# Weight gradient stage: x rows first in tiles, twenty full tiles, score gradients turned by the crossbar

## The chip, the cores and the metric

One core of one Trainium2 chip. The metric is device time in microseconds (us) of the whole kernel, median of several executions. All runs below were in the fast state, and every output was correct.

## The reference, cut to what matters

A recurrent attention block (A) gated by a SwiGLU block (B), forward and backward: the kernel returns the output and the gradients of x and of eight weights. Each of 64 segments attends over 8 memory rows and its own 32 rows of x, and its memory is the output of the segment before.

```python
# B=1, S=2048, Dm=640, H=32 heads of 128, M=8 memory rows, seg=32
for s in range(n_seg):
    h = jnp.concatenate([mem, xs], axis=1)          # 40 rows
    q, k, v = [jnp.einsum('btd,dhe->bhte', h, W) for W in (Wq, Wk, Wv)]
    scores = jnp.where(mask, jnp.einsum('bhqe,bhke->bhqk', q, k) * scale, -1e9)
    o = jnp.einsum('bhqk,bhke->bhqe', softmax(scores), v)
    o = jnp.einsum('bhte,hed->btd', o, Wo)
    mem = o[:, :M, :]
...
_out, _vjp = jax.vjp(_f, A_x, A_mem0, A_Wq, A_Wk, A_Wv, A_Wo, B_w1, B_w3, B_w2)
```

The stage of interest comes after the backward recurrence, when P (the probabilities) and dS (the score gradients) of every tile lie in DRAM. It needs the gradients of the v, k and q rows, with them the gradients of Wv, Wk and Wq, and the gradient of the rows of x. The gradient of the memory rows was already needed inside the recurrence, so computing it here again is waste.

## The kernel before

The stage goes over eight groups of four heads (called "quarters" here and in the recorded texts, though there are eight), each with 22 tiles (three segments, 24 memory rows and then 96 rows of x; the last tile has one segment). A pair of quarter and tile is a unit. To turn is to transpose. Per unit: s1 turns dS on TensorE; s2(i) makes the gradient rows r6p of v, k and q (i = 0, 1, 2) in two rotating banks of PSUM (the memory that TensorE writes; a bank is free again when ScalarE or VectorE has emptied it, below an eviction), and the third needs the turned dS (dST); s3 turns these rows (t6g) into a ring; s4 multiplies each full window of 128 rows by the weights (g). After the 22 units, wg makes the three weight gradients from all tiles and from hr, the rows that the heads were computed from.

```python
def s1(u):
    for j in range(4):
        nc.tensor.transpose(pt[:, j, :], dS[0:n, j, :], k.ident[0:n, 0:n])
    nc.vector.tensor_copy(dST[0:n, :, 0:n], pt[0:n])
def s2(u, i):
    pr = pa.tile([P, 512], F32, name="r6p", tag=bank("s", 3, 2))      # banks 3 and 4
    ...                                                               # four products
    # emptied by ScalarE (i = 0, 2) or VectorE (i = 1) into gr
...
for tl in range(NTL):
    u = u0 + tl
    if tl + 4 < NTL: ld(u + 4)
    if tl + 2 < NTL: s2(u + 2, 0); s2(u + 2, 1)
    if tl + 3 < NTL: s1(u + 3)
    if tl + 1 < NTL: s3(u + 1, 0, 2)
    if tl + 2 < NTL: s2(u + 2, 2)
    if tl + 1 < NTL: s3(u + 1, 2, 3)
    s4(u)
...
```

In the timelines of this case each engine's instructions stand in the written order. The queues differ in what issues them: SP issues most loads and all wg stores, ScalarE the g rows' loads (one a unit, between its evictions), GpSimd the memory rows' loads.

Of the kernel before, what the change touches and what calls it, by code (L numbers as in the profile page):

```python
# [16 lines left out]
P = 128  # L17
# [23 lines left out]
class K:  # L41
# [76 lines left out]
    def build_masks(self, pool, scr):  # L118
        nc = self.nc
        GE = ALU.is_ge  # L120
        n, nm = 120, 24
# [7 lines left out]
        for (c0, w) in ((0, 8), (nm, 32)):  # L129
            v1 = a1[:, c0:c0 + 3 * w].rearrange("p (s c) -> p s c", c=w)  # L130
            v2 = a2[:, c0:c0 + 3 * w].rearrange("p (s c) -> p s c", c=w)
            sel(v1, 1, 0, [[-8, 3], [0, w]])
            sel(v1, -1, 7, [[8, 3], [0, w]])
            sel(v2, 1, -nm, [[-32, 3], [0 if w == 8 else -1, w]])
            sel(v2, -1, nm + 31, [[32, 3], [0, w]])
# [8 lines left out]
        sel(b1[:], -1, 7, [[0, 40]])  # L144
        sel(b2[:], 1, 0, [[-1, 40]])
# [6 lines left out]
    def setup_dram(self):  # L152
# [17 lines left out]
        self.GXA = mk("GXA", (self.NR, D))  # L170
# [23 lines left out]
        for tl in range(self.NTL):  # L194
            n = self.geo(tl)[3]
            self.PR.append(mk(f"PR{tl}", (n, H, n)))
            self.DSR.append(mk(f"DSR{tl}", (n, H, n)))
            ns, nm = self.geo(tl)[0:2]
            self.VTD.append(mk(f"VTD{tl}", (P, ns, H, 40)))
        self.PM = mk("PM", (T, P, 80))  # L200

# [25 lines left out]
    def m_src(self, tl, w, c0, c1):  # L227
        g = c0 // 1024
        out, t = [], 3 * tl
        end = t + self.geo(tl)[0]  # L230
        while t < end:
            e = min(end, t - t % 4 + 4)
            XS = self.store(w)[t // 4, g, 0:8, t % 4:t % 4 + e - t]
            for i in range(2 if w == "qv" else 1):
                X = XS[:, :, i] if w == "qv" else XS
                out.append((8 * (t - 3 * tl), 8 * (e - 3 * tl), X[:, :, c0 - 1024 * g:c1 - 1024 * g].rearrange("r t c -> t r c"), i))
            t = e
        return out
# [6 lines left out]
    def m_rows(self, A, t):  # L245
        r = 120 * (t // 3) + 8 * (t % 3)
        return A[r:r + 8, :]

    def x_rows(self, A, X, eng):
        n = self.NTL - 1  # L250
        eng.dma_start(A[0:120 * n, :].rearrange("(t r) d -> t r d", r=120)[:, 24:120],
                      X[0:96 * n, :].rearrange("(t r) d -> t r d", r=96))
        eng.dma_start(A[120 * n + 8:self.NR, :], X[96 * n:self.S, :])


    def x_pieces(self, A, x0, x1):
        out, a = [], x0
        while a < x1:
            tl = a // 96
            b = min(x1, 96 * tl + 96)  # L260
            r = 120 * tl + self.geo(tl)[1] + a - 96 * tl
            out.append((a - x0, b - x0, A[r:r + b - a, :]))
            a = b
        return out
# [103 lines left out]
def phase3_Afwd(k, W4, Wv, Wk_):  # L368
# [30 lines left out]
    with tc.tile_pool(name="ast", bufs=1) as st, tc.tile_pool(name="achain", bufs=1) as ch, \  # L399
# [174 lines left out]
        def ld(w, tl, qd, eng=nc.sync):  # L574
# [4 lines left out]
            k.load_x(r, nm, k.x_src(tl, w, c0, c0 + 512), eng)  # L579
# [11 lines left out]
        def scores(tl, qd):  # L591
# [8 lines left out]
            for j in range(4):  # L600
                kv = kT[:, h0 + j, 0:n].rearrange("p (s c) -> p s c", c=40)
                nc.tensor.matmul(sp[:, j, 0:nm], qT[:, j, :], kv[:, :, 0:8], start=False, stop=True,
                                 skip_group_check=True)
                nc.tensor.matmul(sp[:, j, nm:n], qT[:, j, :], kv[:, :, 8:40], start=False, stop=True,
# [19 lines left out]
        def norm(tl, qd, eng=nc.gpsimd, q=nc.gpsimd):  # L624
# [6 lines left out]
            q.dma_start(k.PR[tl][:, h0:h0 + 4, :], Pb[0:n, :, 0:n])  # L631
# [19 lines left out]
        def pv(tl, qd, q=nc.gpsimd):  # L651
# [3 lines left out]
            if 4 * tl < k.NO:  # L655
                pt = ps.tile([P, 4, 96], F32, name="xot", tag="x", bufs=5)
                for j in range(4):
                    nc.tensor.matmul(pt[:, j, :], v[0:n, j * P:(j + 1) * P], PTs[qd % 2][0:n, j, 24:120], start=True, stop=True)
# [126 lines left out]
def phase3b_out(k, Wo, W0, W4):  # L785
# [12 lines left out]
    with tc.tile_pool(name="oio", bufs=1) as io, tc.tile_pool(name="oac", bufs=1, space=bass.MemoryType.PSUM) as pa, \  # L798
# [6 lines left out]
        def ld(b, qd):  # L805
# [3 lines left out]
            if nt == 3:  # L809
                src = k.OR[120 * tl:120 * tl + 360, c0:c0 + 512].rearrange("(t r) c -> r t c", r=120)[24:120]  # L810
            else:
                nm, n = k.geo(tl)[1], k.geo(tl)[3]
                src = k.OR[120 * tl + nm:120 * tl + n, c0:c0 + 512].rearrange("(t r) c -> r t c", t=1)
# [82 lines left out]
        while g0:  # L896
# [6 lines left out]
    later = [(k.GWO[0:120 * n, :].rearrange("(t r) d -> t r d", r=120)[:, 24:120], k.GS[0:96 * n, :].rearrange("(t r) d -> t r d", r=96)),  # L903
             (k.GWO[120 * n + 8:k.NR, :], k.GS[96 * n:k.S, :])]

    for s in range(3):
# [3 lines left out]
        for b in range(2):  # L910
            r0 = 120 * tl0 + 8 * s
            dst = k.HRO[120 * tl0:120 * tl0 + 120 * (n - 1), :].rearrange("(t r) d -> t r d", r=120)[:, 8 * s:8 * s + 8]
            r1 = 120 * (tl0 + n - 1) + 8 * s
# [3 lines left out]
            later.append((k.HRO[r1:r1 + 8, cols], k.FS[t1, 32 * b:32 * b + 8, :]))  # L917
# [6 lines left out]
def phase4_Abwd(k, out2, WoT, WvT, WkT, WqT, later):  # L924
# [3 lines left out]
    with tc.tile_pool(name="gst", bufs=1) as st, tc.tile_pool(name="gchain", bufs=1) as ch, \  # L928
# [6 lines left out]
        bdf = st.tile([P, 16, 8], BF16, name="bdf")  # L935
        b16 = st.tile([P, 16], F32, name="b16")
        nc.gpsimd.memset(bdf[:], 0.0)
        nc.gpsimd.affine_select(out=bdf[:], in_=bdf[:], compare_op=ALU.not_equal, fill=1.0, base=0,
                                pattern=[[-1, 16], [-16, 8]], channel_multiplier=1)
        nc.vector.tensor_reduce(b16[:], bdf[:], axis=AX.X, op=ALU.add)  # L940
        nc.vector.tensor_copy(bdm[:], bc_last(b16[:], 8))
        goxs = [st.tile([P, DC, 32], BF16, name=f"gox{i}") for i in range(2)]
        gOTs = [st.tile([P, 4, P], BF16, name=f"gOT{i}") for i in range(2)]
        gors = [st.tile([120, 512], BF16, name=f"gor{i}") for i in range(NG)]
        for tt in goxs + gOTs + gors:
# [53 lines left out]
        def chain(t, gap):  # L999
# [76 lines left out]
            with nc.allow_non_contiguous_dma(reason="mem rows of dS"):  # L1076
                for a in range(2):
                    for (c0, c1, d0) in ((0, 8, 8 * s), (8, 40, nm + 32 * s)):
                        (nc.sync, nc.gpsimd)[a].dma_start(k.DSR[tl][8 * s:8 * s + 8, 16 * a:16 * a + 16, d0:d0 + c1 - c0],
# [16 lines left out]
        def ld(tl, qd, eng=None):  # L1096
# [7 lines left out]
            if g < NG:  # L1104
                gor = gors[g][:]
                qv = fl.tile([120, 2, 512], BF16, name="gqv", tag="gqv", bufs=4)[:]
                Pr = fl.tile([120, 4, n], BF16, name="gPr", tag="gPr", bufs=4)[:]
            else:
# [3 lines left out]
                Pr = x[:, 1536:1536 + 4 * n].rearrange("p (h c) -> p h c", h=4)  # L1112
            if gnm.get(g, 0 if g < NG else 1) != 0 and (g >= NG or gnm[g] < nm):
                nc.vector.memset(gor[0:24, :], 0.0)
# [3 lines left out]
            k.load_x(qv, nm, k.x_src(tl, "qv", c0, c0 + 512), nc.sync)  # L1118
            k.load_x(gor, nm, k.g_src(tl, c0, c0 + 512), nc.scalar if early and i > 3 else nc.sync)
# [3 lines left out]
        def turn(tl, qd):  # L1123
# [7 lines left out]
            nc.scalar.copy(vTq[:, :, :, 0:8].rearrange("p s h c -> p h s c"), pt[:, :, 0:nm].rearrange("p h (s c) -> p h s c", c=8))  # L1131
            nc.scalar.copy(vTq[:, :, :, 8:40].rearrange("p s h c -> p h s c"), pt[:, :, nm:n].rearrange("p h (s c) -> p h s c", c=32))
# [8 lines left out]
        def dprob(tl, qd):  # L1141
# [3 lines left out]
            for j in range(4):  # L1145
                nc.tensor.matmul(dp[:, j, 0:nm], gOT[:, j, :], vTq[:, :, j, 0:8], start=True, stop=True)
                nc.tensor.matmul(dp[:, j, nm:n], gOT[:, j, :], vTq[:, :, j, 8:40], start=True, stop=True)
            uu["d", tl, qd] = dp

        def dsoft(tl, qd):  # L1150
# [5 lines left out]
            dS = fl.tile([120, 4, n], BF16, name="gdS", tag="gdS", bufs=2)  # L1156
            for j in range(4):
                nc.vector.tensor_tensor_reduce(dS[0:n, j, :], dp[0:n, j, :], Pr[0:n, j, :], 1.0, 0.0, ALU.mult, ALU.add,
                                               Dx[0:n, j:j + 1])
            for j in range(4):  # L1160
                nc.vector.scalar_tensor_tensor(dS[0:n, j, :], dp[0:n, j, :], Dx[0:n, j:j + 1], Pr[0:n, j, :],  # L1161
# [4 lines left out]
        def gmem(tl, qd):  # L1166
# [5 lines left out]
            for j in range(4):  # L1172
                nc.tensor.matmul(pk[:, 0, j, :], qv[0:n, 0, j * P:(j + 1) * P], dS[0:n, j, 0:nm], start=True, stop=True)
                nc.tensor.matmul(pk[:, 1, j, :], gor[0:n, j * P:(j + 1) * P], Pr[0:n, j, 0:nm], start=True, stop=True)
# [15 lines left out]
        cnt = dict(l=0)  # L1190
# [83 lines left out]
def phase6_Awgrads(k, X, out0, out3, out4, out5):  # L1274

    nc, tc = k.nc, k.tc
    D, DC, S, H, HD, T, NTL = k.D, k.DC, k.S, k.H, k.HD, k.T, k.NTL
    outf = [o.rearrange("d h e -> d (h e)") for o in (out3, out4, out5)]
    out0f = out0.flatten_outer_dims()
    NW = k.NR // P  # L1280
    R = 384
    with tc.tile_pool(name="h6i", bufs=3) as io, tc.tile_pool(name="h6", bufs=1) as hp, \
            tc.tile_pool(name="h6g", bufs=1) as gp, tc.tile_pool(name="h6a", bufs=1, space=bass.MemoryType.PSUM) as pa:
        start = len(nc.cur_bb.bb.instructions)
        hr = hp.tile([120, NTL, D], BF16, name="hr")
        acc = X.tile([P, NW, D], F32, name="ghacc", tag="x")
        NB = 3
        dSs = [hp.tile([120, 4, P], BF16, name=f"dS6{i}") for i in range(NB)]
        Prs = [hp.tile([120, 4, P], BF16, name=f"P6{i}") for i in range(NB)]
        dSTs = [hp.tile([120, 4, P], BF16, name=f"dST6{i}") for i in range(2)]  # L1290
        ring = hp.tile([P, 3, 4, R], BF16, name="gT6")
        for i, tt in enumerate(dSs + Prs + dSTs):
            (nc.gpsimd, nc.vector)[i % 2].memset(tt[:], 0.0)
        units = [(qd, tl) for qd in range(8) for tl in range(NTL)]
        st, Ws, cnt = {}, {}, dict(w=0, s=0, x=0, g=0)
# [15 lines left out]
        def ld(u):  # L1311
# [4 lines left out]
            nc.sync.dma_start(dS[0:n, :, 0:n], k.DSR[tl][:, h0:h0 + 4, :])  # L1316
            nc.sync.dma_start(Pr[0:n, :, 0:n], k.PR[tl][:, h0:h0 + 4, :])
            rw = []
            for nm_ in ("g", "q", "k"):
                r = io.tile([120, 512], BF16, name="r6", tag=f"r6{nm_}")  # L1320
                src = k.g_src(tl, c0, c0 + 512) if nm_ == "g" else k.x_src(tl, nm_, c0, c0 + 512)
                k.load_x(r, nm, src, nc.scalar if nm_ == "g" else nc.sync)
# [4 lines left out]
        def s1(u):  # L1327
            qd, tl = units[u]
            n = k.geo(tl)[3]
            dS = st["l", u][0]  # L1330
            pt = pa.tile([P, 4, n], BF16, name="t6", tag=bank("x", 5, 3))
            for j in range(4):
                nc.tensor.transpose(pt[:, j, :], dS[0:n, j, :], k.ident[0:n, 0:n])  # L1333
            dST = dSTs[u % 2]
            nc.vector.tensor_copy(dST[0:n, :, 0:n], pt[0:n])  # L1335

        def s2(u, i):
            qd, tl = units[u]
            n = k.geo(tl)[3]
            dS, Pr, rw = st["l", u]  # L1340
            lh = (Pr, dS, dSTs[u % 2])[i]
            rh = rw[i]
            pr = pa.tile([P, 512], F32, name="r6p", tag=bank("s", 3, 2))
            for j in range(4):
                nc.tensor.matmul(pr[:, j * P:(j + 1) * P], lh[0:n, j, :], rh[0:n, j * P:(j + 1) * P], start=True, stop=True)  # L1345
# [563 lines left out]
```

## Time and profile before

| | before |
|---|---|
| median (range), us | 5568.7 (5560.69 to 5575.1) |
| span of the profiled run, granted clock | 5562.0, 0.952 |
| end of the last sum before the stage | 3380.3 |
| from there to the first wg product | 153.7 |
| seven quarters, first wg to first wg | 1306.6 (mean 186.7) |
| last wg groups | 71.6 |
| rest of the kernel | 649.7 |

The rows below the span add up to it within 0.1 us; they are times of instructions in the trace (the first is the end of the last product on the summed fsum, the others are starts of wg products), and the same five are compared for the other kernels. Beyond what the prediction shows, two lines of the transfers view of one quarter (3720.7 to 3905.6 us, from the second start of wg to the third) will be needed. The first counts packets; the second gives a load of 160 KB into 128 partitions (eo_s, rows for the output) and its median time from issue to landing in us.

```profile
DMA packets 42747, 18.25 MB, mean 99 GB/s; under 512 B 33828, under 2 KB 42156, under 8 KB 42730
...
eo_s<-SR POOLq DMA_DIRECT2D x2, 160.0 KB, 2.9
```

Most packets are small: 960 pieces of 240 B for each unit's dS and P.

### The profile page before, as it was taken

To read this page: it belongs to the slowest core of one execution; us is meant where nothing else is said; L and a number is where in the kernel's file an instruction comes from. 1 tells how busy PE (TensorE), PEld (TensorE's weight loads), DVE (VectorE), ACT (ScalarE), POOL (GpSimd) and SP (SyncE) were. 2 spreads that over 40 slices of the span, in tenths; PEclk is the share of its full clock that TensorE was granted. 3 is DMA by queue.
4 is the path that set the end of the run, shared out by engine and by line. 5 is a ranking of instruction groups with operands and counts; after the bars stand their busy time and mean duration, and the time that the engine had idled before them with its cause. 6 is when DMAs were issued, how large, how long until landed. Compare 5 with 4: busy or idle time off the path is not lost. (4 is left out here: it accounts for less than half of the span.)

```text
span 5562.0 us, 164947 instructions
## 1 busy us (share of the span) xinstructions
PE 4935.7 (89%) x66673; PEld 3152.5 (57%) x67020; DVE 2343.2 (42%) x7398; ACT 1783.4 (32%) x4953; POOL 1570.4 (28%) x2604
## 2 busy tenths in 40 slices
PE   4987888888888677989999997999999999998999
PEld 2554555555555444656666665566556655666665
DVE  5833555555555323444444542233223322311451
ACT  2422555555555322323333332233113312300111
POOL 0000344444444212333333333243224322310000
PEclk9998999999999778999999998999999999999999
DMA  7553455555555686666666666354335433657332
GB/s 252 171 185 90 137 152 153 158 156 162 153 151 143 152 171 155 176 186 184 186 184 178 185 169 130 76 124 99 94 74 126 98 87 83 162 166 188 106 117 92
DMA packets 1126617, 808.27 MB, mean 145 GB/s; under 512 B 672971, under 2 KB 1016679, under 8 KB 1123179
## 3 DMA queue, kind: packets, MB, share of 16 engines
q1 hardware_dynamic: 884995, 555.06, 37.3%
q0 software_dynamic: 91472, 144.46, 9.3%
q10 hardware_dynamic: 149388, 98.17, 6.3%
q8 instruction: 529, 8.67, 0.7%
q14 instruction: 233, 1.91, 0.1%
HBM read 468.47 MB, written 296.78 MB: 138 GB/s over the span
## 5 line engine op out<-in xcount | busy, mean ns | idle before, releaser
L1403 PE MATMUL wg<-gr,hr 120*128 120x512 bf16 (+1 forms) x2640 | 592.9, 386 | 17.3 <-DVE dST L1335 13.1
L1381 PE MATMUL g<-w,gT 128*128 128x320 bf16 x3840 | 548.4, 299 | 0.0
L1403 PEld LDWEIGHTS <-hr 120*128 120x128 bf16 (+1 forms) x2640 | 258.9, 99 | 343.1 <-issue 52.1
L1381 PEld LDWEIGHTS <-gT 128*128 128x128 bf16 x3840 | 368.8, 98 | 136.3
L243 POOL DMA_DIRECT2D r<-GOS x256 | 143.4, 564 | 795.8 <-PE r6p L1345 704.8
L90 DVE CAST wgo<-wg 128x512 bf16<-128x512 f32 x72 | 47.5, 688 | 589.2 <-issue 281.8
L316 PEld LDWEIGHTS <-hx 128*32 128x32 bf16 x7680 | 179.7, 97 | 169.4 <-issue 12.4
L90 DVE CAST stg<-bank 128x512 bf16<-128x512 f32 x256 | 177.0, 692 | 208.4 <-PE bank L316 199.4
L335 PEld LDWEIGHTS <-gkv 128*8 128x8 bf16 x8192 | 189.7, 87 | 107.4 <-DVE gkv L1012 23.8
L619 ACT ACTIVATE xP<-xsp,xnm 120x120 bf16<-120x120 f32 (+1 forms) x704 | 240.5, 376 | 8.5 <-DVE xnm L615 4.5
L1390 DVE TENSOR_TENSOR ghacc<-ghacc,g 128x320 f32<-128x320 f32 x240 | 117.0, 487 | 277.7 <-PE g L1381 277.7
L92 ACT CAST wgo<-wg 128x512 bf16<-128x512 f32 x48 | 25.8, 589 | 640.3 <-PE wg L1403 640.3
L1163 POOL DMA_DIRECT2D DSR<-gdS x176 | 101.6, 577 | 426.5 <-DVE gdS L1161 383.3
L1348 ACT CAST gr<-r6p 120x512 bf16<-120x512 f32 (+1 forms) x176 | 103.3, 587 | 361.7 <-PE r6p L1345 340.8
L668 POOL DMA_DIRECT2D OR<-xv x163 | 94.6, 580 | 418.9 <-ACT xv L667 287.0
L92 ACT COPY gT<-t6g 128x960 bf16<-128x960 bf16 (+5 forms) x216 | 167.0, 792 | 119.9 <-PE t6g L1364 117.0
L630 POOL TENSOR_TENSOR xP<-xP,xrz 120x480 bf16<-120x480 bf16 x163 | 161.8, 992 | 141.0 <-ACT xP L619 96.5
L1161 DVE SCALAR_TENSOR_TENSOR gdS<-gdp,Dx,gPr 120x120 bf16<-120x120 f32 (+1 forms) x680 | 182.7, 330 | 0.0
L1232 PE MATMUL gbank<-WqT,ident 128*128 128x512 bf16 x453 | 159.5, 402 | 20.1 <-issue 12.2
L335 PE MATMUL bank<-Wo,oTm 128*32 128x320 bf16 x4032 | 177.0, 329 | 0.1
L316 PE MATMUL gbank<-WoT,gox 128*32 128x512 bf16 x2560 | 153.6, 387 | 24.6 <-POOL gox L967 21.2
L1364 PE MATMUL t6g<-ident,gr 120*128 120x120 bf16 (+1 forms) x2112 | 172.0, 221 | 3.3 <-DVE wgo L90 2.7
(339 smaller groups left out, 10991.0 us busy)
## 6 DMA issues: line engine op xcount, KB each, us to landing
QVS<-stg SPq DMA_DIRECT2D x128, 256.0 KB
gqv<-QVS SPq DMA_DIRECT2D x108, 192.0 KB
vTt<-VTD SPq DMA_DIRECT2D x64, 320.0 KB
VTD<-gvT POOLq DMA_DIRECT2D x168, 120.0 KB, 3.6
OR<-xv POOLq DMA_DIRECT2D x163, 120.0 KB, 2.5
DSR<-gdS POOLq DMA_DIRECT2D x168, 112.5 KB, 3.4
dS<-DSR SPq DMA_DIRECT2D x168, 112.5 KB
P<-PR SPq DMA_DIRECT2D x168, 112.5 KB
```

Of the source, the lines that this page charges most:

```text
L90: return nc.vector.tensor_copy(out, in_)
L92: return nc.scalar.copy(out, in_)
L243: eng.dma_start(d, src if src.shape[0] > 1 else src[0])
L316: k.nc.tensor.matmul(bank[32 * g:32 * g + 32, :], x[:, dc, :], W[:, dc, c0:c0 + 512], start=(dc == 0), stop=(dc == k.DC - 1), tile_positio ...
L335: k.nc.tensor.matmul(pm[p0:p0 + nq, 0:320], x[:, h, :], W[:, h, 320 * b:320 * b + 320], start=(first and i == 0), stop=(last and i == 15), ...
L619: nc.scalar.activation(Pb[0:n, j, 0:n], sp[0:n, j, :], ACT.Exp, bias=nmx[0:n, j:j + 1], scale=k.scale, accum_out=Z[0:n, j:j + 1])
L630: eng.tensor_tensor(Pb[0:n, :, 0:n], Pb[0:n, :, 0:n], bc_last(rz[0:n], n), ALU.mult)
L1161: nc.vector.scalar_tensor_tensor(dS[0:n, j, :], dp[0:n, j, :], Dx[0:n, j:j + 1], Pr[0:n, j, :], op0=ALU.subtract, op1=ALU.mult)
L1232: nc.tensor.matmul((bA if g in ("W1", "G1", "G2") else bB)[:], k.ident[:], WqT[:, 0, 0:512], start=True, stop=True)
L1364: nc.tensor.transpose(pt[:, i - i0, j, :], st["g", u, i][0:n, j * P:(j + 1) * P], k.ident[0:n, 0:n])
L1381: nc.tensor.matmul(pg[:], ring[:, i, j, r0:r0 + P], Ws[qd][i][:, j, 320 * h:320 * h + 320], start=(i == 0 and j == 0), stop=(i == 2 and j ...
L1403: nc.tensor.matmul(accs[dc][:], hr[0:n, tl, dc * P:(dc + 1) * P], st["g", NTL * qd + tl, i][0:n, :], start=(tl == 0), stop=(tl == NTL - 1))
```

## The change

The intent: compute the rows' gradient for the 2048 rows of x only (16 windows instead of 20), feed wg with 20 tiles of 128 rows instead of 22 of 120, and take the turns of dS from TensorE: a transposing transfer of the DMA engines, from SBUF to SBUF, makes them (the crossbar turn). For this, x rows come first in each tile; dS and P are stored padded to 128 columns (one piece of 1024 B a row instead of four of 240); tiles 20 and 21 go first and their 160 rows are stored to DRAM (GSP) and loaded back as rows 120 to 127 of the twenty others, in the fifth unit of a quarter (`p == 4`). The new layouts reach into earlier stages, with the same order of work on TensorE there. The core, with cuts marked:

```diff
+        def dturn(u):
+            dST = io.tile([P, 4, P], BF16, name="dST6", tag="dST6", bufs=4)
+            turned_load(k, dST[:], st["l", u][0][:].rearrange("p j c -> p (j c)"))   # crossbar, SP queue
-        def s1(u): ...        # turn by TensorE
-        def s2(u, i): ...
+        def s2(u):            # the three groups in a row
+            for i in range(3): ...
+                if tl >= NF:
+                    nc.gpsimd.dma_start(k.GSP[qd, i, r0:r0 + n, :], gr[0:n])
+        def spill(qd):
+            for i in range(3):
+                nc.gpsimd.dma_start(grs[i][120:P, :, :], k.GSP[qd, i].rearrange("(t r) c -> r t c", r=8))
...
-            for tl in range(NTL):
-                n = k.geo(tl)[3]
+            for tl in range(NF):                                    # wg: 20 tiles of 128 rows
...
+        ld_to(4); dturn(1)
+        nc.scalar.dma_start(hr[0:120], ...)                         # 3 MB; before: after the loads of unit 2
+        nc.scalar.dma_start(hr[120:P], ...)
...
+                if p + 3 < NTL:
+                    s2(u + 3)
+                    ld_to(u + 3 + NB)                               # loads five units ahead, was two
+                dturn(u + 4)
+                if p + 2 < NTL:
+                    s3(u + 2)
+                s4(u)
+                if p == 4:
+                    spill(qd)
```

## The prediction

> **What bounds the kernel now.** I read the page first for the engine that is busy, then split the span by stages, then cut the weight gradient stage (3398 to 4912 us, 1514 us, the only stage whose TensorE program the change alters) into its eight equal quarters, one for each group of four heads, then read one unit of work in the timeline, and last the waits. From the page:
>
> ```profile
> PE 4935.7 (89%) x66673; PEld 3152.5 (57%) x67020; DVE 2343.2 (42%) x7398; ACT 1783.4 (32%) x4953; POOL 1570.4 (28%) x2604
> ...
> L1403 PE MATMUL wg<-gr,hr 120*128 120x512 bf16 (+1 forms) x2640 | 592.9, 386 | 17.3 <-DVE dST L1335 13.1
> L1381 PE MATMUL g<-w,gT 128*128 128x320 bf16 x3840 | 548.4, 299 | 0.0
> ...
> L1364 PE MATMUL t6g<-ident,gr 120*128 120x120 bf16 (+1 forms) x2112 | 172.0, 221 | 3.3 <-DVE wgo L90 2.7
> ```
>
> TensorE is the busy engine, and the two costliest groups of the whole kernel, the weight gradient product (wg) and the rows' gradient (g), are both in this stage; neither waits much. The windows view of one quarter, from the first wg product to that of the next quarter:
>
> ```profile
> 3905.61:4090.45 184.84, 176.10 (x1428) 114.27 (x1426) 57.27 (x124) 47.87 (x77) 57.54 (x104) 0.97 0.42 99
> ```
>
> Columns: window, length, busy us (instructions, in merged rows) of PE, PEld, DVE, ACT, POOL, clock, DMA share, GB/s. PE is busy 95% of a quarter, every other engine under 35%, DMA 42%. Seven such quarters last 184.6 to 189.4 us, mean 186.7 (4840.73 - 3534.07 over 7). So TensorE's order of work sets the time. One unit (a tile of three segments, four heads) in the timeline of TensorE:
>
> ```profile
> 4003.86 0.39 PE L1345 MATMUL r6p<-r,P 120*128 120x128 bf16 x4
> 4004.08 0.39 PE L1345 MATMUL r6p<-r,dS 120*128 120x128 bf16 x4
> 4004.31 0.37 PE L1333 MATMUL t<-ident,dS 120*128 120x120 bf16 x4
> 4004.52 0.58 PE L1364 MATMUL t6g<-ident,gr 120*128 120x120 bf16 x8
> 4004.94 0.39 PE L1345 MATMUL r6p<-r,dST 120*128 120x128 bf16 x4
> 4005.16 0.37 PE L1364 MATMUL t6g<-ident,gr 120*128 120x120 bf16 x4
> 4005.37 3.42 PE L1381 MATMUL g<-w,gT 128*128 128x320 bf16 x24
> 4008.63 0.39 PE L1345 MATMUL r6p<-r,P 120*128 120x128 bf16 x4
> ```
>
> Start to start: 0.22 us for four products of 128 columns, 0.21 for four turns of dS (t), 0.63 for twelve turns of the gradient rows (t6g), 3.26 for the 24 products of one g window; 4.77 in all, without a gap. Note that turns and t6g stand between the second r6p group and the third. The r6p results rotate through two PSUM banks, so the third needs the bank of the first, after ScalarE has emptied it. The same three groups without anything between them occur between the wg groups:
>
> ```profile
> 3957.92 0.38 PE L1345 MATMUL r6p<-r,P 120*128 120x128 bf16 x4
> 3958.14 0.39 PE L1345 MATMUL r6p<-r,dS 120*128 120x128 bf16 x4
> 3958.34 0.59 ACT L1348 CAST gr<-r6p 120x512 bf16<-120x512 f32 x1
> 3958.98 0.38 PE L1345 MATMUL r6p<-r,dST 120*128 120x128 bf16 x4 [0.45 <-ACT gr L1348]
> ```
>
> There the third starts 1.06 us after the first instead of 0.45: 0.61 us lost (the bracket says 0.45, because a group's modelled end is later than its last issue).
>
> **What the Trainium skill says.** "TensorE: Matmul & The Clock Gate", section "Wait — 56ns, not 53.3ns?", gives N / 2.4 GHz + about 2.5 ns per warm matmul. The trace agrees: 3.26 us / 24 = 136 ns at 320 columns, 0.63 / 12 = 52.5 ns at 120. So the turns pay for their columns, not for their weights, and 96 columns should take about 42.5 ns (estimate). "Perfetto Trace Analysis", section "Matmuls", says that independent groups should rotate through banks so that the emptying of one overlaps the next; the 1.06 us above shows what two banks for three groups cost. "DMA: Bandwidth & Descriptors", section "Specifications", asks for at least 512 B a transfer: the dS and P loads here land as four 240 B pieces a row and become one of 1024 B. Its section "Latency and other measured facts" gives 261 GB/s for a DMA transpose; 128 KB would be 0.5 us of the queues (estimate from that page; no run here has a turn from SBUF).
>
> **The change part by part.** All per quarter, from the durations above; the order of TensorE's program before this stage is unchanged, row by row.
> - Rows' gradient for x rows only: 2048 rows are 16 windows of 128 instead of 20. 4 x 3.26 = -13.0.
> - Weight gradients over 20 full tiles instead of 22 of 120 (one short): 30 products fewer of 512 columns at 24.0 / 110 = 0.218: -6.5.
> - Turns of dS go to the crossbar: 22 x 0.21 = -4.6, and 0.4 us of VectorE each, which was hidden.
> - t6g with 96 columns: 12 x 10 ns x 22 = -2.6 (estimate from the rate).
> - Waits of the turns for dS loads: from 3604 to 4830 us TensorE waited 15.3 us for dS<-DSR, 6.6 quarters, so 2.3 each. Loads now run five units ahead over the quarter's edge: -2.3.
>
> That is -29.0. What is added on the same path:
> - The new order has all three r6p groups in a row (the compiled order of the changed kernel shows it: third group waits for ScalarE), still with two banks. 17 units of the steady loop, 0.61 each: +10.4. It does not hide: TensorE is in order, and what follows waits behind it.
> - 16 windows over 22 units leave every fourth unit without g products. There ScalarE has two casts (0.59, 0.60) and a copy of 768 columns (about 0.8, from 0.96 at 960) against 1.8 us of TensorE, so the next unit's first cast starts late. Worked through by hand, the third group then starts 1.55 after the first, 0.49 more than 1.06; four such units: +2.0.
> - Between the wg groups one r6p group more queues behind the wgo casts: +2.0 (judged from 2 to 2.7 us waits there now).
>
> Net -29.0 + 14.4 = -14.6 a quarter, x 8 = -117. The spill of the last two tiles (six small stores, three loads of 8 rows) has some 80 us before wg reads it: hidden. The start of the stage (41 us until the first g product, DMA at 0.9 to 1.15) has the same bytes to load: 0. The other stages keep their order; whole-row stores of P, and one load instead of two or three in the last stage, are worth a few us at most. I give back 10 us for the new queue (below): 5564 - 107 = 5457.
>
> **Rivals.** (1) The saving shows in full: the stall is hidden by TensorE's queue. Then -29 x 8 = -232, about 5330. Against it is the measured 1.06 us with ScalarE idle before. (2) The crossbar turn comes late. It is issued when the unit two before has left TensorE, and after four loads of about 0.4 us on the same queue; its result is needed about 9.8 us later, 6.5 where a unit without a window lies between. Loads take some 3 to 4 us here, so there is room, but at the quarter's edges (DMA 0.96 to 1.05 while the w turns run) it may fail. One us in every unit would be 176 us and leave the kernel slower than before; I think a few waits at the edges more likely, and that is the 10 us. (3) DMA becomes the bound: 42% now, fewer pieces for dS and P, one crossbar transfer more; the share should stay under 55%. (4) ScalarE's backlog spreads: its work is 48 us of 185, so it recovers in each window; against.
>
> **Range and chances.** The terms removed are sure to some 15 us; the stall count is sure, its size 0.5 to 0.7 (plus or minus 20 us); the edges plus or minus 30. Range 5410 to 5505. The 2% line is 5453, a few us under my number, so it is near even: faster 0.46, same 0.53, slower 0.01.
>
> **What would show it.** A steady unit with a window should take 5.05 us instead of 4.77 (longer, though it does less), with r6p<-dST waiting about 0.45 for ACT on line of the cast; units without a window near 1.8; g 3072 products, wg 2400, no t group; wg 64.7 a quarter; quarters near 172. In the waits, DMA dS<-DSR gone as TensorE's releaser, ACT the largest one, some 80 us in the idle column over the stage. I am wrong if r6p<-dST waits for a DMA of dST in the steady loop, if t6g still takes 0.63, if the third group starts under 0.7 us after the first, or if a stage before 3398 moves by over 15 us.

## The result, and the profile after

5610.23 us median (5604.01 to 5615.36), against 5568.7 before: ratio 1.0075 (0.0019 either way at 95%), where 5457 was predicted. All ratios here are the mean time of one kernel's fast runs over that of the other's of the same rounds, so not quite the ratio of the medians. The page of the profiled run, its busy times and its costliest groups of the stage:

```profile
PE 4787.0 (85%) x64913; PEld 3029.7 (54%) x65308; DVE 2245.6 (40%) x7110; ACT 1758.4 (31%) x4913; POOL 1562.8 (28%) x2675
...
L1344 PE MATMUL r6p<-r,dST 120*128 120x128 bf16 (+1 forms) x704 | 74.7, 234 | 224.6 <-DMA dST<-dS 121.3
```

TensorE does 149 us less and the kernel is 47 us longer: the third r6p group has 225 us of idle time before it. The parts of the span, against before: the first part +15.3 (3395.6), from there to the first wg +21.8 (175.5), seven quarters +15.4 (1322.0, where 102 less were predicted), last wg groups -7.1, rest +1.4. The seven quarters are six of 182.7 to 187.0 and a last of 209.1. Who held TensorE from 3398 to 5000 us (total us, times, longest), from the waits view:

```profile
PE r6p L1344 <- DMA dST<-dS: 121.3, 30, 7.9
PE r6p L1344 <- ACT gr L1351: 69.0, 128, 2.8
PE r6p L1344 <- ACT grs L1351: 34.1, 12, 28.8
PE r6p L1344 <- DMA r<-KS: 16.3, 1, 16.3
```

The second line is the stall that was predicted (16 a quarter). The first is the late crossbar turn, which was given 10 us. The last two are, but for 5 us, single long waits at the start of the stage. One such turn in the timeline of the sixth quarter:

```profile
4413.35 0.39 PE L1344 MATMUL r6p<-r,P 120*128 120x128 bf16 x4
4413.58 0.39 PE L1344 MATMUL r6p<-r,dS 120*128 120x128 bf16 x4
4414.41 0.38 PE L1344 MATMUL r6p<-r,dST 120*128 120x128 bf16 x4 [0.45 <-ACT gr L1351]
4414.64 0.68 PE L1374 MATMUL t6g<-ident,gr 96*128 96x96 bf16 x12
4415.15 3.42 PE L1389 MATMUL g<-w,ghacc 128*128 128x320 bf16 x24
...
4426.53 0.61 PE L1344 MATMUL r6p<-r,dST 120*128 120x128 bf16 x4 [7.51 <-DMA dST<-dS]
4426.94 1.17 PE L1374 MATMUL t6g<-ident,gr 96*128 96x96 bf16 x12
4427.90 5.48 PE L1389 MATMUL g<-w,ghacc 128*128 128x320 bf16 x24
```

The first five lines are a steady unit exactly as foretold: 5.06 us from start to start, 0.45 of waiting in it. The unit after it waits 7.51 us for its turn, and then everything runs at a lower rate: twelve t6g turns 1.17 instead of 0.68, a g window 5.48 instead of 3.42. That is what the Trainium skill, "TensorE: Matmul & The Clock Gate", section "What's actually happening", calls the cold state, half clock after an idle window of about 3.4 us; this trace agrees: all 16 of the 30 waits that were 3.9 us or longer are followed by slow products. This wait cost 2.7 us more than its own length (the unit took 14.82 us, 9.76 over a steady one, where the wait of 0.45 became one of 7.51). The windows view from the second start of wg to the third shows that the DMA engines do more than the prediction's 55%:

```profile
3756.80:3941.80 185.00, 154.74 (x1208) 97.69 (x1212) 45.21 (x89) 44.66 (x72) 62.72 (x113) 0.94 0.62 121
```

(last three columns: clock, DMA share, GB/s; before 0.97, 0.42, 99). And the transfers view of the same stretch:

```profile
DMA packets 39881, 22.47 MB, mean 121 GB/s; under 512 B 25592, under 2 KB 39043, under 8 KB 39866
...
gr<-GSP POOLq DMA_DIRECT2D x3, 160.0 KB, 11.6
...
eo_s<-SR POOLq DMA_DIRECT2D x2, 160.0 KB, 4.9
```

The three spill loads into eight partitions take 11.6 us each where 160 KB into 128 partitions took 2.9 before, and now takes 4.9. Fewer packets are small (25592 against 33828), since dS and P come in whole rows; without the turns it would be 13624, as the first experiment shows.

### The profile page after: what moved, and what is told of

The parts are those of the page before. It is cut to its first block, busy times and chain, and to the rows that moved or that the text cites. A ratio compares the mean times of both kernels' runs of the same rounds, so it can differ in the third digit from the quotient of the medians.

```text
span 5608.7 us, 161247 instructions
## 1 busy us (share of the span) xinstructions
PE 4787.0 (85%) x64913; PEld 3029.7 (54%) x65308; DVE 2245.6 (40%) x7110; ACT 1758.4 (31%) x4913; POOL 1562.8 (28%) x2675
## 5 line engine op out<-in xcount | busy, mean ns | idle before, releaser
L1410 PE MATMUL wg<-gr,hr 128*128 128x512 bf16 x2352 | 532.6, 386 | 16.5 <-DVE grs L1353 7.6
L1389 PE MATMUL g<-w,ghacc 128*128 128x320 bf16 x3072 | 471.8, 314 | 0.0
L1410 PEld LDWEIGHTS <-hr 128*128 128x128 bf16 x2400 | 237.9, 99 | 305.0 <-issue 35.8
L1389 PEld LDWEIGHTS <-ghacc 128*128 128x128 bf16 x3072 | 309.8, 103 | 129.9
L1344 PE MATMUL r6p<-r,dST 120*128 120x128 bf16 (+1 forms) x704 | 74.7, 234 | 224.6 <-DMA dST<-dS 121.3
L1398 DVE TENSOR_TENSOR ghacc<-ghacc,g 128x320 f32<-128x320 f32 x192 | 93.7, 488 | 251.0 <-PE g L1389 251.0
L1344 PEld LDWEIGHTS <-dST 120*128 120x128 bf16 (+1 forms) x704 | 55.0, 103 | 247.4 <-DMA dST<-dS 151.1
L1351 ACT CAST gr<-r6p 120x512 bf16<-120x512 f32 x160 | 94.0, 588 | 295.1 <-PE r6p L1344 294.9
```

The costliest lines, as they stand in the source:

```text
L1344: nc.tensor.matmul(pr[:, j * P:(j + 1) * P], lhs[i][0:n, j, :], rw[i][0:n, j * P:(j + 1) * P], start=True, stop=True)
L1389: nc.tensor.matmul(pg[:], ring[:, i, j, r0:r0 + P], Ws[qd][i][:, j, 320 * h:320 * h + 320], start=(i == 0 and j == 0), stop=(i == 2 and j ...
L1410: nc.tensor.matmul(accs[dc][:], hr[:, tl, dc * P:(dc + 1) * P], grs[i][:, tl, :], start=(tl == 0), stop=(tl == NF - 1))
```

## The experiments

Each edit is against the changed kernel. The table lists the result of each as a ratio to the kernel before, and in per cent of it what that is against the changed kernel (1.0075). 0.1% is 5.6 us. The four calls shared their runs of before, whose medians were 5568.0, 5580.3, 5573.1 and 5570.0. The 95% intervals of these ratios reach 0.0017 to 0.0038 either way, so differences under some 0.4% between two rows of the table are not sure.

| run | edit to the changed kernel | median, us | ratio to before | against changed |
|---|---|---|---|---|
| e_peturn | dS turned by TensorE | 5511.88 | 0.9909 | -1.7 |
| e_early | crossbar turn issued 2 units earlier | 5604.33 | 1.0080 | 0.0 |
| e_order | third r6p group after 8 turns | 5574.37 | 1.0018 | -0.6 |
| e_gxa | last-quarter stores off SP | 5577.7 | 1.0025 | -0.5 |
| e_hr | hr later, GpSimd | 5607.05 | 1.0049 | -0.3 |
| e_spill | spill loads spread | 5590.2 | 1.0023 | -0.5 |
| e_x_all | crossbar + all five mends above | 5578.33 | 0.9995 | -0.8 |
| e_x_sp | e_x_all + g rows on SP | 5494.64 | 0.9870 | -2.0 |
| e_pe_order | TensorE turn + order | 5482.06 | 0.9830 | -2.4 |
| e_pe_late | e_pe_order, spill loads together, later | 5484.98 | 0.9842 | -2.3 |
| e_pe_spill | e_pe_order + spill spread | 5432.59 | 0.9751 | -3.2 |
| e_pe_row | e_pe_spill without order | 5479.55 | 0.9838 | -2.4 |
| e_pe_all | e_pe_spill + hr later | 5433.8 | 0.9748 | -3.3 |
| e_pe_first | e_pe_all + other tiles first | 5428.5 | 0.9745 | -3.3 |
| e_pe_dummy | e_pe_all + idle crossbar turns | 5507.73 | 0.9893 | -1.8 |
| e_pe_gsp | e_pe_spill + g rows on SP | 5410.49 | 0.9719 | -3.6 |

### Turn dS on TensorE again

```diff
         def dturn(u):
-            turned_load(k, dST[:], st["l", u][0]...)
+            for j in range(4):
+                nc.tensor.transpose(pt[:, j, :], st["l", u][0][:, j, :], k.ident[:])
+            nc.vector.tensor_copy(dST[:], pt[:])
```

> Only the crossbar turn is undone: the score gradients are turned by TensorE again (four 128x128 products into PSUM, one VectorE copy, issued where the crossbar turn was issued). Theory 1 (late crossbar turns ate the gain): the 121 us of TensorE's waits r6p<-dST for a DMA and the slow products behind them go, the turns cost 176 x 0.21 = 37 us of TensorE, so 85 to 120 us less than the changed kernel (5610), about 5490 to 5525, below the kernel before. Theory 2 (the ScalarE stall of three r6p groups in a row is the whole loss): the dST waits were hiding it, and the time stays within 30 us of 5610 or rises by the 37. In both the start of the stage keeps its 21 us over before.

5511.88, ratio 0.9909. In the range of theory 1: about 92 us come back (0.0166 of 5568) though TensorE does 704 products more, 0.22 us a unit from start to start, 39 in all. The first line is from the waits from 3398 to 5000 us, the second from its transfers between the second start of wg and the third:

```profile
PE r6p L1347 <- ACT gr L1354: 96.9, 148, 5.1
```
```profile
DMA packets 27913, 19.58 MB, mean 109 GB/s; under 512 B 13624, under 2 KB 27075, under 8 KB 27898
```

No wait for dST is left; the wait for ScalarE, which the late turns had probably covered in part, grows from 69 to 97. Against the changed kernel 11,968 small packets are missing from a quarter: 544 a turn. The kernel was now faster than before, so the crossbar turn was more than the whole loss. The padded rows of dS and P stay in this version, so they are not what made the kernel slower. How the turn costs was open.

### Issue the crossbar turn earlier

```diff
+                if p < NTL - 2:
+                    dturn(u + 6)
                 if p + 3 < NTL:
                     s2(u + 3)
                     ld_to(u + 3 + NB)
-                dturn(u + 4)
```

> Only the time of issue of the crossbar turns is changed: each is put on the SP queue two units (about 10 us) earlier, ahead of the unit's stores and loads; same work. Theory 1 (the turn is late because it is issued late and lands up to 12 us later): the r6p<-dST waits for a DMA fall from 121 us to under 30, and with the slow clock behind them the time falls by 90 to 130 us to 5480 to 5520. Rival (the queue or the transfers themselves are saturated, so that earlier turns only delay the loads): the waits move to r6p<-dS or r6 loads and the time stays within 20 us of 5610. Theory 2 (ScalarE stall): waits r6p<-gr for ACT rise above today's 69 us as the dST waits no longer cover them, to about 85.

5604.33, ratio 1.0080: nothing, against the time that theory 1 gave; it is the time of the rival, though the waits moved elsewhere than the rival said. The waits for dST did go, all but 0.6 us. Their place was taken. From TensorE's waits from 3398 to 5000 us, and ScalarE's and SP's from 3560 to 4890:

```profile
PE r6p L1344 <- ACT gr L1351: 178.3, 142, 9.3
```
```profile
ACT ghacc L92 <- DMA dST<-dS: 46.3, 14, 9.5
ACT ghacc L92 <- DMA r<-GOS: 40.4, 8, 8.6
```
```profile
SPq L272 <- DMA dS<-DSR: 175.8, 124, 8.8
```

How to read this: ScalarE's copy into the ring needs no transfer. It stands in ScalarE's program behind the issue of a load (r<-GOS), and that issue waited for some earlier transfer's landing, a crossbar turn in 14 cases. ScalarE's evictions stood behind it, and TensorE behind those. The last line is the turn's own issue: two units earlier it comes before the load of its dS has landed, so SP stood there, and with it the loads behind it in SP's program; in the changed kernel this wait is not among SP's seventeen longest (all over 2.6 us). So theory 1 in its first form, a turn that is only issued too late, fell: earlier turns moved the wait.

### The order of the groups

```diff
+                if i == 2 and mid is not None:
+                    mid()                        # s3(u + 2), first eight turns
                 pr = pa.tile([P, 512], F32, name="r6p", ...)
```

> Only the order inside a unit is changed: the third r6p group comes after the first eight turns of the unit before, as in the kernel before. Theory 2 (stall for ScalarE's eviction): the 69 us of waits r6p<-gr for ACT fall under 10 and the time falls by 55 to 75 us to 5535 to 5555. Theory 1: the third group also needs dST 0.35 us later, so dST waits fall by at most 0.35 x 30 = 10 us, and stay above 105; gain of the whole under 80. Rival: the stall was hidden behind something else, and the time moves by under 20 us.

5574.37, ratio 1.0018: 32 us (0.0057 of 5568), not 55 to 75. ScalarE's line went from 69.0 to 7.7, as expected, but half of the gain was given back: ScalarE's other cast came to 13.0 us of waits, those for dST rose from 30 to 46 (121.3 to 127.1 us), and the g products were busy 479.1 us instead of 471.8, in more time at the slow clock.

### The last quarter's stores

```diff
-                    nc.sync.dma_start(k.GXA[P * w:P * w + P, :], gx[:])
+                    nc.gpsimd.dma_start(k.GXA[P * w:P * w + P, :], gx[:])
```

> Only the 16 stores of the finished rows' gradient in the last quarter leave the SP queue for GpSimd's. Theory 1 for the last quarter (these stores wait on SP for the sum and hold the turns and loads behind them): the last quarter's 209 us fall to about 188, the dST waits by 25 to 32 us, and the time by 18 to 30 us, to 5580 to 5592. Rival (the last quarter is long for its own VectorE work or for the transfers of the stage after it): under 8 us change.

5577.7, ratio 1.0025: 28 us, inside the range of theory 1. The last quarter fell from 209.1 to 184.0, like the others. In the changed kernel SP waited at these stores for the sums, and the turns and loads behind them in its queue waited too:

```profile
SPq L1400 <- DVE gxo L1398: 70.1, 16, 7.7
```

Before, these stores stood on SP as well, but no turn stood behind them.

### The first load of hr

```diff
-        nc.scalar.dma_start(hr[0:120], ...)       # at the start of the stage
+                if qd == 0 and p in (6, 8, 10, 12):
+                    nc.gpsimd.dma_start(hr[0:120, a:a + 5], ...)
```

> Only the loads of hr (3 MB, used first 100 us later) leave ScalarE's queue at the start of the stage: they go in five pieces on GpSimd's queue in units 6 to 14 of the first quarter. If these loads caused the late start (SP waited 17.8 us for one of them, ScalarE's first eviction came 40 us later than in the kernel before), the time from the last sum of the stage before to the first product wg falls from 175 us by 15 to 25 us and the whole to 5585 to 5597. Rival (the start waits for the mem rows' and score gradients that the stage before has only just written, whatever hr does): under 8 us.

5607.05, ratio 1.0049. A miss: from the last sum to the first wg it took 172.7 us, 2.8 less. The 16.3 us wait for r<-KS and the 28.8 for grs were gone, and the waits for dST rose to 152.2. The ratio's 15 us are not seen in its profile, and its interval (1.0022 to 1.0076) meets that of the changed kernel (1.0056 to 1.0093), so it stays open whether hr gave anything here; with the TensorE turn it gave nothing (e_pe_all against e_pe_spill: in one profile of each, the start of the stage is 9 us shorter and the seven quarters are 9 us longer).

### The parts together, with and without the crossbar

Three kernels: TensorE turn and group order; these with hr later and the spill loads spread (the edit below); and the crossbar with this and all the single mends above.

```diff
-                if p == 4:
-                    spill(qd)                      # three loads at once
+                if p in (4, 9, 14):
+                    spill(qd, p // 5)              # one at a time
```

> Two parts undone together: TensorE turns the score gradients, and the third r6p group comes after eight turns of the unit before. With the TensorE turn alone the time was 5512 and 96.9 us of TensorE waited for ScalarE's eviction of gr. If this stall is on the path once no turn is late, it falls under 15 us and the time by 55 to 85 us, to 5427 to 5457, at least 2% under the kernel before. Rival (about half of such a saving is given back, as with the crossbar, where 69 us of stall gone made 35): 5465 to 5485.

5482.06, ratio 0.9830: 44 us under e_peturn, less than the 55 to 85 expected, and inside the range of the rival. 43.7 us of waiting for ScalarE were left, in 21 waits of up to 5.6 us.

> The same two parts undone, with hr loaded in pieces in the first quarter on GpSimd's queue, and the three spill loads spread over units 4, 9 and 14 of each quarter. If the start of the stage and the spill loads still cost once no crossbar turn depends on them: 15 to 30 us less than with the two parts alone. Rival (their cost was only through the crossbar turns' queue): under 8 us for both.

5433.8, ratio 0.9748: 46 us less, more than the 15 to 30 expected. This is 2.5% under before.

> The crossbar turn is kept and all else is mended: issued two units earlier, the third r6p group after eight turns, last-quarter stores and hr on GpSimd's queue, spill loads spread. If only the place of issue made the turns late, the sum of the single runs plus the dST waits: 5610 - 35 - 30 - 20 - 60 = 5465 or less, level with the version that turns on TensorE or better, as TensorE's 37 us are saved. If the turns cost by loading the 16 DMA engines (share 0.62 against 0.45 with the TensorE turn), so that loads land later and hold ScalarE and SP: 5500 to 5540, at least 40 us over the TensorE version.

5578.33, ratio 0.9995: level with before, 38 us over even the worst number expected, and 138 us (in ratio) over the kernel with the TensorE turn, e_pe_all; the second expectation had the sign right and the size too small. TensorE waited 127.2 us for ScalarE's first cast (from 3398 to 5000 us). Both e_hr and e_early had shown waits that move; here it is the whole. This kernel holds the early turns too, at which SP stands; the other mends with the turn issued late were not run together. ScalarE's waits from 3560 to 4720:

```profile
ACT gr L1353 <- DMA dST<-dS: 66.0, 19, 5.7
ACT gr L1353 <- DMA r<-GOS: 53.4, 13, 5.8
```

### Is it the load or the wait?

The fastest kernel so far, with crossbar turns that nobody reads:

```diff
             nc.vector.tensor_copy(dST[:], pt[:])
+            dum = io.tile([P, 4, P], BF16, name="dum", tag="dum", bufs=4)
+            turned_load(k, dum[:], st["l", u][0][:].rearrange("p j c -> p (j c)"))
```

> The fastest version so far (turn on TensorE, group order, hr and spill loads spread: 5434) with the crossbar turns added back as idle work: issued where the changed kernel issues them, into a tile that nothing reads. TensorE never waits for their result. If the crossbar turns cost by their load on the DMA engines and queues (loads land later and hold ScalarE, SP and the next loads): 50 us or more over 5434, with TensorE waiting for ScalarE's gr or for loads r. If they cost only where TensorE waits for the turned tile: within 15 us of 5434.

5507.73, ratio 0.9893 against 0.9748 without: 81 us for transfers whose result no engine needs, over the 50 of the first expectation. The windows of one quarter, from the third start of wg to the fourth, without them (first fence) and with them (second), then TensorE's wait from 3398 to 5000 us:

```profile
3886.30:4052.80 166.50, 155.36 (x1296) 101.75 (x1300) 52.47 (x111) 43.87 (x72) 62.77 (x113) 0.98 0.48 118
```
```profile
3910.00:4084.70 174.70, 158.34 (x1303) 102.46 (x1301) 52.51 (x111) 43.82 (x72) 62.57 (x113) 0.96 0.65 129
```
```profile
PE r6p L1351 <- ACT gr L1358: 85.5, 38, 6.2
```

The DMA share goes from 0.48 to 0.65: (0.65 x 174.7 - 0.48 x 166.5) / 22 = 1.5 us of all 16 engines a turn, three times the 0.5 that the prediction worked out. Counted by size in these two stretches of the traces, a turn is 512 packets of 256 B and 32 of 4 B, whose own time is about 1.1 us of all 16 engines; the rest is other transfers' packets that take longer (those of 1024 B on SP's queue 69 ns instead of 61). TensorE's wait for ScalarE goes from 27.5 to 85.5. Whether the engines' load or the place on SP's queue does the harm is not told apart by this run; both belong to the turn.

Then ScalarE's part in it. The crossbar kernel with everything mended, and the g rows' loads issued by SP:

```diff
-                k.load_x(r, 0, src, nc.scalar if nm_ == "g" else nc.sync)
+                k.load_x(r, 0, src, nc.sync)
```

> The crossbar version with all else mended (5578, 127 us of TensorE waiting for ScalarE's gr), with the loads of the g rows moved from ScalarE's queue to SP's. If ScalarE is late because its queue must wait for a transfer before it can issue its load (73 us of its first eviction's idle time ended by a crossbar turn's landing), the 127 us fall under 30 and the time by 60 to 100 us, to 5480 to 5520. If the DMA engines are the limit, the wait moves to loads and turns (r6p<-dST or <-r for a DMA over 80 us) and the time stays within 25 us of 5578.

5494.64, ratio 0.9870 against 0.9995: 70 us in ratio, 84 in medians, in the range of the first theory. TensorE's wait for ScalarE's first cast fell from 127.2 us to 3.5, but that for dST rose from 14.3 to 74.5, beside 20.6 for r, so that the wait in part moved as the second theory said:

```profile
PE r6p L1346 <- DMA dST<-dS: 74.5, 43, 10.1
PE r6p L1346 <- DMA r<-GX: 20.6, 7, 5.5
```

So both theories hold a part: some 70 us were ScalarE being held at its own load issue, and the rest of the distance to the TensorE turn (0.9870 against 0.9751 or less) stays with the crossbar (the early turns among it), although its steady unit is the shortest of all, 4.72 us.

### Spill loads and the start

The spread of the spill loads shown above, alone on top of the TensorE turn and the group order:

> The turn on TensorE and the group order undone (5482), and only the spill loads spread over units 4, 9 and 14; hr stays where the change put it. Of the 46 us between 5482 and 5434, if the spill loads made them (one wait of about 5 us for ScalarE in each quarter near unit 6, with slow products behind it): 5440 to 5452. If hr made them (12 us seen at the start of the stage): 5465 to 5480.

5432.59, ratio 0.9751: below the range for the spill loads, so that they made all of the 44 us and hr none.

All three together, in another place:

```diff
-                if p == 4:
+                if p == 14:
                     spill(qd)
```

> Turn on TensorE and group order (5482), with all three spill loads kept together but in unit 14. If their being three at once costs, wherever they stand: within 12 us of 5482. If their place in unit 4 costs, just after the eo loads and the first loads of the quarter, and they are harmless where less is in flight: 5430 to 5445, as when spread.

5484.98, ratio 0.9842, as in unit 4 (0.9830). It is their being three at once, in either place. Spread, each lands in 6.1 us instead of the 9.7 of e_pe_order, by the transfers of one quarter of e_pe_spill:

```profile
gr<-GSP POOLq DMA_DIRECT2D x3, 160.0 KB, 6.1
```

The changed kernel itself, with the spread alone:

> The changed kernel with one edit: the three spill loads of a quarter go in units 4, 9 and 14 instead of all in unit 4. In the changed kernel units 8 to 10 of a quarter take 6 to 9 us more than steady ones, in which the spill loads are in flight. If the three together make that: 35 to 60 us less than the changed kernel (5610), 5550 to 5575. If the crossbar turns wait there anyway, for the eo loads and the next rows: under 15 us.

It gives 5590.2, ratio 1.0023: about 29 us, but the interval (0.9985 to 1.0060) is wide and just meets that of the changed kernel; between both expectations. dST waits fell from 121.3 to 102.0.

And, on top of e_pe_all, other tiles first:

```diff
-        units = [(qd, tl) for qd in range(8) for tl in order]
+        order0 = [NF, NF + 1] + list(range(4, NF)) + list(range(4))
+        units = [(qd, tl) for qd in range(8) for tl in (order if qd else order0)]
```

> The fastest version so far (5434) with the first quarter's units in another order: tiles 4 to 19 ahead of 0 to 3, since the rows of tile 0 are the last that the stage before writes. If the start waits for just-written rows (TensorE waited 12.4 and 8.5 us at the first units): 12 to 22 us less, 5412 to 5422. If the start waits for the first loads of any rows: within 6 us of 5434.

5428.5, ratio 0.9745 against 0.9748: no difference. The first units do not wait for rows just written.

### The stall, and the best version

The version of e_pe_spill with the group order of the changed kernel (the edit of "The order of the groups" taken back):

> The version with the turn on TensorE and spread spill loads (5433), with the three r6p groups in a row again. Predicted size of the stall: 0.61 us x 17 units x 8 quarters = 83 us, less what the four VectorE and TensorE instructions of the turn between cover. If the stall is on the path in full: 5505 to 5520; if half of it is given back as between 5512 and 5482: 5460 to 5475.

5479.55, ratio 0.9838 against 0.9751: 48 us, above the range for "half given back" and below that for the full stall. The reason is in the units: steady 5.28 us in a row and 4.94 interleaved, so the reorder saves 0.34 and not 0.61. The unit of the best version shows where the rest is. It is e_pe_spill with the g rows' loads on SP, the edit of e_x_sp:

> The version with the turn on TensorE, group order and spread spill loads (5433), with the g rows' loads on SP's queue instead of ScalarE's. TensorE still waited 16 us for ScalarE's first eviction there, and 30 us of that eviction's idle time ended with a transfer's landing. If a held ScalarE queue still costs: 10 to 20 us less, 5413 to 5423. If SP's longer queue delays the loads by as much: within 6 us, or slower.

5410.49, ratio 0.9719 (0.9695 to 0.9743): 2.8% under before and 18 us under e_pe_spill in ratio, inside the expected 10 to 20 (the median is 2.5 us below the expected range). The intervals of the two ratios overlap a little; TensorE's wait for ScalarE's first cast, 16.3 us in e_pe_spill, is not among its nine longest, and the seven quarters take 1151.2 us instead of 1175.5. Its sixth quarter in TensorE's timeline:

```profile
4349.15 0.39 PE L1349 MATMUL r6p<-r,dS 120*128 120x128 bf16 x4
4349.37 0.51 PE L1379 MATMUL t6g<-ident,gr 96*128 96x96 bf16 x8
4349.98 0.38 PE L1349 MATMUL r6p<-r,dST 120*128 120x128 bf16 x4
4350.20 0.39 PE L1333 MATMUL t<-ident,dS 128*128 128x128 bf16 x4
4350.43 0.34 PE L1379 MATMUL t6g<-ident,gr 96*128 96x96 bf16 x4
4350.60 3.42 PE L1394 MATMUL g<-w,ghacc 128*128 128x320 bf16 x24
```

Eight turns take 0.34 us (8 x 42.5 ns); the third group starts 0.61 after their start. Some 0.27 are still lost: the third group starts 1.06 us after the first (4348.92, just above these lines), as it does in a row, so the eight turns only fill part of that time. Units of this quarter, start to start in us, from the traces (units 9, 13 and 17 have no g window):

| unit | 6 | 7 | 8 | 9 | 10 | 11 | 12 | 13 | 14 | 18 |
|---|---|---|---|---|---|---|---|---|---|---|
| changed | 5.51 | 5.06 | 14.82 | 1.79 | 5.53 | 5.06 | 5.06 | 1.79 | 5.53 | 5.53 |
| e_x_sp | 5.11 | 4.72 | 5.75 | 2.02 | 5.21 | 5.31 | 5.88 | 3.13 | 7.53 | 8.56 |
| e_pe_gsp | 5.11 | 4.94 | 4.94 | 1.68 | 5.16 | 4.94 | 4.94 | 1.68 | 5.16 | 5.16 |

In the best version the steady units repeat exactly; quarters take 162.5 to 167.0 us. In the crossbar version single units lose 0.5 to 3.5 us all through the quarter.

## Why the prediction was wrong

What it got right, step by step. The removed terms are there: 3072 g products, 16 windows at the unchanged 3.26 us; t6g 0.51 for twelve; the last wg groups 64.5 instead of 71.6. The stall is right to the hundredth: a steady unit 5.06 (5.05 said), without a window 1.79 (1.8), the unit after it 5.53 (5.05 + 0.49). The best version's seven quarters take 1151.2 us against 1306.6, 22 us a quarter less; the removed terms without the turn were put at 24.4 (the best version differs in its loads too).

What failed:

1. "A few waits at the edges more likely, and that is the 10 us" (rival 2, crossbar turn late). This is the step that failed. The waits were 121.3 us in 30 places. Most of it, 86 us, was at units 4 and 8 of a quarter (unit 8 is the first after the three spill loads), and 22 us at other units of the last quarter. Behind 20 of the 30 the products ran at the slow clock, which the prediction did not have: the g products were busy for 471.8 us, and 441.3 in e_pe_spill, which hardly waits, 30 us more for the same 3072 products. Leaving the turn on TensorE gave back 92 us, although it costs TensorE 39. The rival was named with its size (176), and given too small a share: a turn's own time was taken from a rate (0.5 us), and a turn measured about 1.1 us of all engines, 1.5 with what it does to other transfers. A sign that the prediction named came with it: r6p<-dST waited for a DMA of dST in the loop. In the parts of the span the miss of 154 us (profiled runs) is 118 in the seven quarters and 30 at the start of the stage, where 8 of the first quarter's gain were due, less the 10 kept back, and 15 before the stage.
2. "Hidden" for the spill. The data was needed 80 us later, that part is right; but three loads into eight partitions at once delayed the transfers beside them. With the TensorE turn this cost 44 us, and about 29, less surely, with the crossbar. These gains overlap: e_x_all has all the mends, and not their sum.
3. "The start of the stage: 0". It took 21.8 us longer, with two waits of 28.8 and 16.3. Moving hr took these two away and the dST waits grew in their place; what causes the start's loss is not settled. In e_pe_gsp the start takes 155.3, as before.
4. The last quarter was not looked at by itself. Its stores of finished rows hold SP's queue, where turns now stand: 28 us.

"A stage before 3398 moves by over 15 us": it moved by 15.3. Over the changed kernel and its variants, whose programs agree up to there, its end lies between 3374.9 and 3402.2, so no effect of the change is shown in it.

The other theories: the ScalarE stall (theory 2) is real and not the cause of the miss, since it was in the sum; removing it alone gave 32 us. The DMA-bound rival (3) was dismissed on a share under 55%; it was 62%, and the idle turns show that it mattered. Not separated: the load of a turn on the engines from its place on SP's queue. A crossbar turn that is issued late, with g rows on SP and the other mends, was not run.

## What to carry to other kernels

Work taken off the bound engine and given to a transfer is not free if that transfer's result is on the path of an in-order engine: measure the transfer's own cost by issuing it idle before counting on it. When an early issue removes a wait and the time stays, look for the next engine that is held: one whose program mixes evictions with load issues, or the issuing one itself, which may now stand before its input has landed. Spread slow, narrow transfers in time even when their data is needed much later.

## What the Trainium skill lacked or had wrong

- "Advanced Engine Details and Errata", section "X-Bar Transpose (TRN2)", has crossbar transposes as fast as regular DMAs, and "DMA: Bandwidth & Descriptors", section "Latency and other measured facts", gives 261 GB/s. Here, among the other transfers of a quarter, a turn of 128 KB within SBUF was 544 packets under 512 B, whose own time was about 1.1 us of all 16 engines (some 120 GB/s, an estimate from the packets of e_pe_dummy against e_pe_all); with the slowing of other transfers it cost 1.5 us (some 85 GB/s).
- "Perfetto Trace Analysis", section "DMA Optimizations", suggests balancing DMAs across sync, scalar and GpSimd when descriptor generation is the limit. It lacks the other side: an engine that evicts PSUM is held when its load issue waits for another transfer. Moving one load a unit off ScalarE gave 18 us here with the TensorE turn and 70 with the crossbar, both in ratio.
- "DMA: Bandwidth & Descriptors" tells how many engines a transfer of few partitions gets, but has no measured time for several such at once: 160 KB into 8 partitions landed in 9.7 us when three went together, in 6.1 one at a time, and 2.9 us was seen for 160 KB into 128 partitions in the kernel before; the grouping cost 44 us.
